# A gated mix of a recurrent attention block and a GEGLU block: one projection group fewer, and all items of a segment in a new order

## The chip, the cores and the metric

The kernel runs on one core of a Trainium2 chip. The time is the device time of one execution in microseconds, as the median of several runs. The profile is one further execution taken with the hardware profiler. PE is TensorE's matmuls and PEld its weight loads, DVE is VectorE, ACT is ScalarE, POOL is GpSimd, and SP only issues DMAs here.

## The reference

`x` has 2048 rows of 640. `g * a + (1 - g) * b` is returned, with `g` a sigmoid gate per row, `b` a GEGLU block (640 to 1536 and back) and `a` an attention that runs over 64 segments of 32 rows. Each segment has 8 memory rows in front, and its new memory comes out of its own attention, so that segment s+1 cannot begin before segment s has ended:

```
for s in range(64):
    h = concat([mem, x[:, 32*s:32*s+32]], axis=1)            # 40 rows
    q, k, v = (einsum('btd,dhe->bhte', h, W) for W in (Wq, Wk, Wv))   # 32 heads of 192
    scores = where(mask, einsum('bhqe,bhke->bhqk', q, k) * 192**-0.5, -1e9)
    o = einsum('bhqk,bhke->bhqe', softmax(scores), v)
    o = einsum('bhte,hed->btd', o, Wo)
    mem = o[:, :8].copy()
    outs.append(o[:, 8:])
```

## The kernel before

A first part (to about 178 us of the span) computes the GEGLU block for all rows, stores `b` in DRAM, loads the attention's weights into SBUF and prepares gates and the first inputs. After it comes `segment(s)` (line 1314) for the 64 segments, all instructions written out.

**Inside a segment.** The 32 heads are taken in four head groups 0 to 3, of eight heads each. The weights of one head group and one matrix are five pieces of 128x1536 (k = 0 to 4). A list `PROG` (line 518) gives the order of the segment's items, and `segment` emits them one by one; each engine runs what it gets in just this order. There is no scheduler: `_Sched` (line 50) only works out which semaphore each instruction must wait for. The items are:

- `("g", n, k)`: row k of projection group n (`proj`, line 1039). `GROUPS` (line 517) says which projections share a group, as pairs of matrix (0 Q, 1 K, 2 V) and head group. For each member there are four matmuls of 384 columns side by side, one for each 32-column strip of the array. All members multiply the same 128x32 input, so only the first member loads weights into the array (line 1061); the others go through `_matmul_kept` (line 226) and keep them. One PSUM bank is taken for each member at k = 0 (`misc_bank`, line 1012, the one longest unused). At k = 4 ScalarE evacuates each member (Q and K at line 1081, V at line 1084), in the group's order. In kind-0 segments (s mod 4 = 0) V is also computed for the rows left over from four segments ("Vl", line 1074).
- `("tq", i)` and `("tk", i)`: VectorE transposes Q or K of head group i (line 1095); for Q, GpSimd makes a copy, Qz (line 1098). There is one buffer for all Q and one for all K.
- `("sc", i)`: mask and scores on TensorE (lines 1106 to 1121), then maximum and subtraction on VectorE (1133, 1135). GpSimd fills in the memory columns of the next head group.
- `("ex", i)`: exponential on ScalarE (1145), sum, reciprocal and products on VectorE (1147 to 1152).
- `("pt", i)`: the probabilities are transposed on TensorE ("pT", lines 1168 and 1173) and evacuated by ScalarE (1186; for the last head group 1180, with VectorE's 1182 beside it).
- `("pv", i)`: the value product on TensorE (1201, 1203), evacuated by ScalarE (1212; the last head group's third part by VectorE, 1217).
- `("wo", i, h)`: half of the output projection of head group i (1230; 1253 for the last group).
- `("lf", q, u, k)` and `("le", q, u, m)`: in segments with s mod 4 = q, Q and K of rows that a later four segments need ("left" rows, line 899), and their evacuation and store (lines 904, 906, 1300, 910). `("vb", k)`: a V row of the same sort, in kind 3 (line 1034).

At the end of a segment VectorE adds up the result and transposes the new memory into the next segment's input (lines 1395, 1399); the next segment's first row waits for that.

**Weights.** Not all weights fit in SBUF. Thirteen pieces of Q, K and V and three of Wo share their places with those of the opposite head group. The head groups are taken forwards in even segments and backwards in odd ones, and as soon as a shared piece has been used for head group 0 (in the order of the segment), SP issues the load of the piece for head group 3 into the same place (`swap_loads`, line 624; 384 KB each, 480 KB for Wo). All DMAs of the segments stand on SP's queue.

The places in the text: "sc2" is the scores of head group 2, "pT2" the first transposing matmul of its probabilities, "K2" its K projection, "the last Wo pairs" line 1253. Head groups are numbered in the segment's own order.

```
    GROUPS = [[(0, 0), (1, 0)], [(2, 0), (0, 1), (1, 1)], [(2, 1), (0, 2)], [(1, 2)], [(2, 2), (0, 3)], [(1, 3)], [(2, 3)]]
    for n, (m, i) in enumerate(ms):                     # in proj: the members of a group
        S_.add("pe", mms(m, bk, htile(k), k, g_, n > 0), ...)   # n > 0: the array's weights are kept
```

Of the kernel before, what the change touches and what calls it, by code (L numbers as in the profile page):

```python
# [238 lines left out]
def _build(nc, A_x, A_mem0, A_Wq, A_Wk, A_Wv, A_Wo, seg_len, w_gate, w_up, w_down,  # L239
# [272 lines left out]
    def piece_view(key, o):  # L512
        if key[0] == 3:
            return bview(o, GO).rearrange("p (c n) -> p c n", n=Dm)
        return bview(o, GQ)

    GROUPS = [[(0, 0), (1, 0)], [(2, 0), (0, 1), (1, 1)], [(2, 1), (0, 2)], [(1, 2)], [(2, 2), (0, 3)], [(1, 3)], [(2, 3)]]
    PROG = [("g", 0, 0), ("g", 0, 1), ("g", 0, 2), ("g", 0, 3), ("g", 0, 4), ("tq", 0), ("g", 1, 0), ("tk", 0),
# [13 lines left out]
    assert NOCT == 4  # L532
    WOP = 4
    NWP = NT
# [4 lines left out]
    def octet(s, i):  # L539
        return i if s % 2 == 0 else NOCT - 1 - i  # L540
# [5 lines left out]
    def seg_order(s):  # L546
        keys = []
        for item in PROG:
            if item[0] == "g":
                keys += [(m, octet(s, i), item[2]) for m, i in GROUPS[item[1]]]  # L550
            elif item[0] == "wo":
# [487 lines left out]
    def proj(s, item):  # L1039
        ms = GROUPS[item[1]]  # L1040
        k = item[2]
# [233 lines left out]

    assert PROG.index(("g", [n for n, ms in enumerate(GROUPS) if (2, 1) in ms][0], KT - 1)) < PROG.index(("wo", 0, 0))
    late_at = ("g", 1, KT - 1)
# [7 lines left out]
    at = PROG.index  # L1285
    k_end, v_end = [max(at(("g", n, KT - 1)) for n, ms in enumerate(GROUPS) if mi in ms) for mi in ((1, NOCT - 1), (2, NOCT - 1))]
    for x, u in mids:
# [26 lines left out]
    def segment(s):  # L1314
# [3 lines left out]
        for n, item in enumerate(PROG):  # L1318
            kind, i = item[0], item[1]
            if kind == "g":  # L1320
# [5 lines left out]
                proj(s, item)  # L1326
                ki = [j for m, j in GROUPS[i] if m == 1 and item[2] == KT - 1]
                kind, i = ("k", ki[0]) if ki else ("", 0)
# [116 lines left out]
def bass_gated_mix__memory_aug_recurrent_mem_tr__glu_gated_geglu__prompt_kernel(  # L1445
    nc,
    A_x,
    A_mem0,
    A_Wq,
    A_Wk,  # L1450
    A_Wv,
    A_Wo,
    A_seg_len,
    B_x,
    B_w_gate,
    B_w_up,
    B_w_down,
    gate_w,
    out,
):  # L1460
    _build(nc, A_x, A_mem0, A_Wq, A_Wk, A_Wv, A_Wo, A_seg_len, B_w_gate, B_w_up, B_w_down, gate_w, out)
# [33 lines left out]
```

## Time and profile before

| | us |
|---|---|
| median of 3 runs (1767.09 to 1770.34) | 1770.06 |
| profiled execution | 1771.21 |
| its span | 1769.4 |
| busy: PE, PEld | 1606.2, 798.4 |
| busy: DVE, ACT, POOL | 959.9, 803.3, 400.6 |
| read from HBM, written | 473.22 MB, 21.11 MB |
| mean busy share of the DMA engines, 130 to 1769 us | 0.80 |
| granted TensorE clock | 0.997 |

A busy PE is not PE at its peak: the ends of matmuls are modelled and overlap. A wait row reads "engine line waited for: us in total, times, longest us". A group row reads "line engine op out<-in xcount | busy us, mean ns of one | idle us before, and what ended it". A timeline row gives start, length, engine, line and operation, and in brackets the idle time ahead of it and what ended that; "issue" means that nothing which the profile shows ended it.

Positions inside a segment are counted from the first matmul of its first projection row. "Kind" is s mod 4; the kinds differ in their left rows and in kind 3's second use of Wo. Instructions of TensorE are counted as matmuls plus weight loads.

### The profile page before, as it was taken

Reading aid. Unit: us, or ns where it says so; the run is one execution under the profiler, and the core shown is the slowest. Engines: PE = TensorE matmul, PEld = TensorE weight load, DVE = VectorE, ACT = ScalarE, POOL = GpSimd, SP = SyncE. Lnnn points to the kernel's source line nnn. Section 1 sums busy time; section 2 is a strip of 40 time slices with the busy share of each in tenths; the row PEclk is TensorE's granted clock in tenths of the full one; section 3 lists DMA queues with packets and bytes.
Section 4 is the critical chain, followed back from the end, with each engine's and each line's share of the span. In section 5 each row is a group of like instructions: output and inputs, shape, how many; then the busy total and the mean of one; then the engine's idle time right before and its main releaser. Section 6 shows DMA issues by size and latency. Waiting matters only on the chain.

```text
span 1769.4 us, 80660 instructions
## 1 busy us (share of the span) xinstructions
PE 1606.2 (91%) x39162; PEld 798.4 (45%) x31501; DVE 959.9 (54%) x2934; ACT 803.3 (45%) x1835; POOL 400.6 (23%) x1358
## 2 busy tenths in 40 slices
PE   9999899989998999889999998988998899989987
PEld 4554444444444444444444444444444444444443
DVE  2222655556565655556555555555565655655554
ACT  3222544545444544445444544444444454444443
POOL 1100222222222222222222222222222222222222
PEclk9999999999999999999999999999999999999999
DMA  9914987888778887878778886878787887879776
GB/s 319 310 45 153 328 314 258 318 306 292 275 271 310 298 312 254 308 289 313 279 273 293 306 314 226 318 283 300 275 284 288 296 315 259 312 276 326 283 277 236
DMA packets 271313, 499.58 MB, mean 282 GB/s; under 512 B 105304, under 2 KB 132208, under 8 KB 270960
## 3 DMA queue, kind: packets, MB, share of 16 engines
q1 hardware_dynamic: 267832, 491.34, 78.2%
q8 instruction: 276, 4.52, 1.0%
q10 hardware_dynamic: 3128, 3.09, 0.5%
q14 instruction: 77, 0.63, 0.1%
HBM read 473.22 MB, written 21.11 MB: 279 GB/s over the span
## 4 chain that ended last, share of the span: by engine, by line
PE 66%; DVE 17%; issue 6%; DMA 5%; ACT 4%; POOL 1%; DVEq 0%; SPq 0%; ACTq 0%; POOLq 0%
PE ps L1061 18%; PE ps L226 14%; PE ps L1230 8%; DMA arena<-in_A_Wo_dram 4%; PE ps L818 3%; PE ps L1201 3%; PE ps L815 3%; PE ps L899 3%; DVE ps L1135 2%; PE ps L1106 2%; DVE arena L1133 2%; PE ps L833 2%; DVE arena L1147 2%; PE ps L1253 2%; DVE arena L1095 2%
## 5 line engine op out<-in xcount | busy, mean ns | idle before, releaser
L1061 PE MATMUL ps<-arena 128*32 128x384 bf16 x9940 | 727.7, 328 | 52.2 <-DVE arena L1399 33.6
L226 PE MATMUL ps<-arena 128*32 128x384 bf16 x7680 | 595.3, 327 | 7.8 <-DVE arena L1239 3.5
L1061 PEld LDWEIGHTS ps<-arena 128*32 128x32 bf16 x9940 | 259.5, 97 | 377.0 <-issue 238.3
L1095 DVE STREAM_TRANSPOSE arena<-arena 128x384 bf16<-128x384 bf16 x512 | 270.6, 557 | 151.3 <-ACT arena L1081 150.3
L1081 ACT ACTIVATE arena<-ps 128x384 bf16<-128x384 f32 x512 | 236.2, 489 | 213.6 <-PE ps L1061 193.2
L1230 PE MATMUL ps<-arena 128*32 128x320 bf16 x6144 | 294.7, 300 | 15.1 <-issue 12.4
L1145 ACT ACTIVATE ps<-ps 104x160 f32<-104x160 f32 x256 | 71.9, 281 | 285.3 <-DVE ps L1135 285.3
L1230 PEld LDWEIGHTS ps<-arena 128*32 128x32 bf16 x6144 | 163.3, 96 | 76.8 <-issue 19.2
L1133 DVE TENSOR_REDUCE arena<-ps 104x4 f32<-104x160 f32 x256 | 82.9, 324 | 163.0 <-PE ps L1121 163.0
L1212 ACT ACTIVATE arena<-ps 128x480 bf16<-128x480 f32 (+1 forms) x256 | 137.0, 535 | 42.5 <-PE ps L1203 37.8
L1098 POOL COPY arena<-arena 64x160 bf16<-64x160 bf16 x256 | 81.3, 318 | 325.3 <-DVE arena L1095 314.2
L1186 ACT ACTIVATE arena<-ps 128x448 bf16<-128x448 f32 x192 | 104.2, 543 | 99.7 <-PE ps L1173 99.1
L1220 POOL COPY arena<-arena 128x96 bf16<-128x96 bf16 x256 | 68.2, 266 | 356.8 <-ACT arena L1212 267.6
L1084 ACT ACTIVATE arena<-ps 128x384 bf16<-128x384 f32 x256 | 125.1, 489 | 26.4 <-PE ps L1061 21.1
L1147 DVE TENSOR_REDUCE arena<-ps 104x4 f32<-104x160 f32 x256 | 83.0, 324 | 93.4 <-ACT ps L1145 93.4
L1201 PE MATMUL ps<-arena 128*64 128x160 bf16 x1536 | 122.1, 242 | 12.1 <-ACT arena L1186 5.8
L1201 PEld LDWEIGHTS ps<-arena 128*64 128x64 bf16 x1536 | 80.8, 109 | 89.1 <-issue 31.6
L899 PE MATMUL ps<-arena 128*32 128x384 bf16 x1280 | 112.7, 332 | 2.4 <-issue 2.4
L956 POOL COPY arena<-arena 128x96 bf16<-128x96 bf16 x256 | 70.3, 275 | 194.1 <-PE ps L1121 130.2
L1203 PE MATMUL ps<-arena 128*64 128x64 bf16 x1536 | 104.8, 194 | 3.9 <-issue 3.9
L1239 DVE TENSOR_TENSOR arena<-ps,arena 64x160 f32<-64x160 f32 x160 | 50.8, 317 | 75.2 <-ACT arena L1236 60.9
L906 DVE STREAM_TRANSPOSE arena<-arena 128x384 bf16<-128x384 bf16 x128 | 73.7, 576 | 31.7 <-ACT arena L904 27.5
(88 smaller groups left out, 2040.7 us busy)
## 6 DMA issues: line engine op xcount, KB each, us to landing
arena<-in_A_Wk_dram SPq DMA_DIRECT2D x335, 384.0 KB, 7.3
arena<-in_A_Wv_dram SPq DMA_DIRECT2D x335, 384.0 KB, 9.1
arena<-in_A_Wo_dram SPq DMA_DIRECT2D x205, 480.0 KB, 6.4
arena<-in_A_Wq_dram SPq DMA_DIRECT2D x209, 384.0 KB, 5.1
arena<-left_qk_scratch SPq DMA_DIRECT2D x126, 96.0 KB, 3.0
left_qk_scratch<-arena SPq DMA_DIRECT2D x49, 192.0 KB, 2.4
left_qk_scratch<-arena SPq DMA_DIRECT2D x30, 96.0 KB, 5.9
ffn_b_scratch<-arena ACTq DMA_DIRECT2D x16, 160.0 KB, 3.8
```

The source lines that it names most:

```text
L226: return e.add_instruction(mybir.InstMatmult(name=nm, start_tensor_calc=like["start"], stop_tensor_calc=stop, tile_size=(128, 32), tile_po ...
L899: fns.append(lambda e, outp=outp, rhs=rhs, j=j: e.matmul(outp, lhs, rhs, start=(k == 0), stop=(k == KT - 1), tile_position=(0, 32 * j)))
L1061: fns.append(lambda e, outp=outp, rhs=rhs, j=j: e.matmul(outp, lhs, rhs, start=(k == 0), stop=(k == KT - 1), tile_position=(0, 32 * j)))
L1081: S_.add("act", lambda e, m=m, bk=bk: e.activation(out=rows_sb[m], in_=ps[:, bk, 0:384], func=ACTF.Copy), reads=[r_ps[bk]], writes=[r_rows ...
L1084: S_.add("act", lambda e, i=i, bk=bk: e.activation(out=v_sb[i % NVB].rearrange("p (c n) -> p c n", c=3), in_=ps[:, bk, 0:384].rearrange("p ...
L1095: S_.add("dve", lambda e: e.transpose(out=dst[:, :, 0:L], in_=rows_sb[m].rearrange("p (c r) -> p c r", r=L)), reads=[r_rows[m]], writes=[r ...
L1133: S_.add("dve", lambda e: e.tensor_reduce(out=mxs, in_=S3, axis=AX.X, op=ALU.max), reads=[rb], writes=[rst], name="smax max")
L1147: S_.add("dve", lambda e: e.tensor_reduce(out=sms, in_=S3, axis=AX.X, op=ALU.add), reads=[rb], writes=[rst], name="smax sum")
L1201: return [lambda e: e.matmul(full, v[:, e0:e0 + 64], PTm[:, i], start=True, stop=False, tile_position=(0, 64 * i), skip_group_check=True), ...
L1203: lambda e: e.matmul(part, vl[:, e0:e0 + 64], PTl[:, i], start=False, stop=True, tile_position=(0, 64 * i), skip_group_check=True)]
L1212: S_.add("act", lambda e: e.activation(out=apx(u[:, 0, 0, :], [[R, na], [3 * R, 4], [1, R]]), in_=ps[:, A, 0:na * W].rearrange("p (c t r) ...
L1230: fns.append(lambda e, i=i, t=t, j=j, gv=gv: e.matmul(ps[32 * j:32 * j + 32, bank, 0:2 * DJ].rearrange("p (h n) -> p h n", h=2), lhs2[i], ...
```

## The change

Two tables change and nothing else. K of head group 2 is no longer a group of its own but the third member of the group with V of head group 1 and Q of head group 2, so that there are six groups instead of seven; it takes a bank at the same time as the other two, and its twenty matmuls run with kept weights. And `PROG` lists all items in a new order. In it "sc" of head group 1 is followed directly by "pv" of head group 0, and "sc" of head group 3 by "pv" of head group 2 (before, "sc" of 2 was followed by "pv" of 1, in kind 1 with a left row between). The rows of V of head group 3 stand nearer to each other, most left rows come earlier, and the last "wo" half is now the last item, so that all "le" items are emitted ahead of the segment's end.

```
-    GROUPS = [[(0, 0), (1, 0)], [(2, 0), (0, 1), (1, 1)], [(2, 1), (0, 2)], [(1, 2)], [(2, 2), (0, 3)], [(1, 3)], [(2, 3)]]
+    GROUPS = [[(0, 0), (1, 0)], [(2, 0), (0, 1), (1, 1)], [(2, 1), (0, 2), (1, 2)], [(2, 2), (0, 3)], [(1, 3)], [(2, 3)]]
     PROG = [("g", 0, 0), ("g", 0, 1), ("g", 0, 2), ("g", 0, 3), ("g", 0, 4), ("tq", 0), ("g", 1, 0), ("tk", 0),
             ("g", 1, 1), ("g", 1, 2), ("sc", 0), ("g", 1, 3), ("ex", 0), ("g", 1, 4), ("tq", 1), ("g", 2, 0),
-            ("g", 2, 1), ("g", 2, 2), ("lf", 1, 0, 0), ("pt", 0), ("g", 2, 3), ("tk", 1), ("g", 2, 4), ("g", 3, 0),
-            ("sc", 1), ("g", 3, 1), ("lf", 1, 0, 1), ("g", 3, 2), ("ex", 1), ("g", 3, 3), ("g", 3, 4), ("g", 4, 0),
-            ("lf", 1, 0, 2), ("pv", 0), ("lf", 1, 0, 3), ("g", 4, 1), ("tk", 2), ("g", 4, 2), ("pt", 1), ("g", 4, 3),
-            ("tq", 2), ("g", 4, 4), ("sc", 2), ("ex", 2), ("lf", 1, 0, 4), ("pv", 1), ("g", 5, 0), ("le", 1, 0, 0),
-            ("g", 5, 1), ("lf", 0, 1, 0), ("g", 5, 2), ("wo", 0, 0), ("le", 1, 0, 1), ("tq", 3), ("pt", 2), ("g", 5, 3),
-            ("wo", 0, 1), ("g", 5, 4), ("pv", 2), ("tk", 3), ("lf", 0, 1, 1), ("lf", 1, 1, 0), ("wo", 1, 0), ("sc", 3),
-            ("lf", 2, 1, 0), ("wo", 1, 1), ("g", 6, 0), ("lf", 2, 1, 1), ("lf", 1, 1, 1), ("g", 6, 1), ("ex", 3),
-            ("g", 6, 2), ("wo", 2, 0), ("lf", 1, 1, 2), ("pt", 3), ("g", 6, 3), ("lf", 2, 1, 2), ("g", 6, 4),
-            ("wo", 2, 1), ("lf", 2, 1, 3), ("lf", 1, 1, 3), ("pv", 3), ("lf", 0, 1, 2), ("lf", 2, 1, 4), ("lf", 1, 1, 4),
-            ("vb", 0), ("le", 1, 1, 0), ("vb", 1), ("vb", 2), ("vb", 3), ("le", 1, 1, 1), ("le", 2, 1, 0),
-            ("lf", 0, 1, 3), ("lf", 0, 1, 4), ("wo", 3, 0), ("le", 2, 1, 1), ("le", 0, 1, 0), ("wo", 3, 1), ("le", 0, 1, 1),
-            ("vb", 4)]
+            ("tk", 1), ("g", 2, 1), ("pt", 0), ("g", 2, 2), ("g", 2, 3), ("g", 2, 4), ("sc", 1), ("pv", 0),
+            ("g", 3, 0), ("tq", 2), ("g", 3, 1), ("g", 3, 2), ("g", 3, 3), ("ex", 1), ("lf", 1, 0, 0), ("tk", 2),
+            ("g", 3, 4), ("lf", 1, 0, 1), ("pt", 1), ("g", 4, 0), ("sc", 2), ("lf", 2, 1, 0), ("ex", 2), ("g", 4, 1),
+            ("lf", 1, 0, 2), ("pv", 1), ("lf", 1, 0, 3), ("lf", 2, 1, 1), ("lf", 1, 0, 4), ("lf", 2, 1, 2),
+            ("g", 4, 2), ("le", 1, 0, 0), ("g", 4, 3), ("tq", 3), ("le", 1, 0, 1), ("lf", 2, 1, 3), ("g", 4, 4),
+            ("tk", 3), ("lf", 0, 1, 0), ("wo", 0, 0), ("wo", 0, 1), ("pt", 2), ("g", 5, 0), ("g", 5, 1),
+            ("lf", 1, 1, 0), ("wo", 1, 0), ("sc", 3), ("pv", 2), ("lf", 1, 1, 1), ("lf", 0, 1, 1), ("g", 5, 2),
+            ("wo", 1, 1), ("ex", 3), ("g", 5, 3), ("lf", 2, 1, 4), ("wo", 2, 0), ("g", 5, 4), ("vb", 0), ("pt", 3),
+            ("lf", 1, 1, 2), ("lf", 0, 1, 2), ("wo", 2, 1), ("pv", 3), ("lf", 1, 1, 3), ("lf", 1, 1, 4),
+            ("lf", 0, 1, 3), ("lf", 0, 1, 4), ("le", 2, 1, 0), ("vb", 1), ("vb", 2), ("vb", 3), ("le", 0, 1, 0),
+            ("vb", 4), ("wo", 3, 0), ("le", 1, 1, 0), ("le", 0, 1, 1), ("le", 1, 1, 1), ("le", 2, 1, 1), ("wo", 3, 1)]
```

All line numbers behind these tables are one smaller in the changed kernel.

## The prediction

> **What bounds the kernel now.** I read the page from the top, then the waits, the groups, the timeline segment by segment, and the order of the instructions in the two programs. On the page:
>
> ```profile
> span 1769.4 us, 80660 instructions
> ...
> PE 1606.2 (91%) x39162; PEld 798.4 (45%) x31501; DVE 959.9 (54%) x2934; ACT 803.3 (45%) x1835; POOL 400.6 (23%) x1358
> ...
> q8 instruction: 276, 4.52, 1.0%
> ...
> PE 66%; DVE 17%; issue 6%; DMA 5%; ACT 4%; POOL 1%; DVEq 0%; SPq 0%; ACTq 0%; POOLq 0%
> ```
>
> TensorE is on two thirds of the chain, VectorE's answers on 17%, and 6% is "issue", where TensorE waits for nothing that the profile shows. From the start of the first segment to that of the last, 63 segments take 1560 us, 24.8 each. I call them kind 0 to 3 by s mod 4; their means are 25.05, 24.88, 23.47 and 25.64 us. Each span starts with Q0's first row. Adding, for each pair of neighbouring items, the shortest spacing of that pair anywhere in the timeline gives TensorE's own work: 21.16, 20.27, 18.55 and 21.11. So some 4.5 us a segment are waits; the order of the items can only move those.
>
> ```profile
> ACT ps L1145 <- DVE ps L1135: 285.3, 256, 3.4
> PEld ps L1061 <- issue: 238.3, 819, 2.6
> PEld ps L1168 <- DVE arena L1152: 82.1, 148, 1.0
> ```
>
> The third row is TensorE's wait for a finished softmax (pT after the last "smax p"). By place, as the mean idle time ahead of an item beyond that shortest spacing, the waits that the new order touches are (kinds 0/1/2/3, us): pT2 .66/.42/.92/.54; sc2 0/.07/.29/.31; sc3 of kind 2 .24; pT0 of kinds 2 and 3 .25; the value product of group 2 in kind 1 .46; the last Wo pairs .06/.53/.54/.17.
>
> The second wait is instruction supply. The 276 packets of queue 8 carry 16 KB each, and 39162+31501 TensorE instructions over 276 are 256: one packet per 256 instructions. Between the first and last segment 75 gaps over 350 ns between matmuls have no semaphore behind them; every one lies at the same place of the 256. One:
>
> ```profile
> 1008.96 0.27 PEld L1061 LDWEIGHTS ps<-arena 128*32 128x32 bf16 x9 [1.29 <-issue]
> ```
>
> No border is passed sooner than 2.18 us after the packet that holds what follows it began. From 3.5 to 18 us of a segment, while 13 weight pieces queue on the DMA rings, that packet begins 3.66 us (median) after a late passing of the border before; after 19 us only 1.2. So in the middle a block costs up to 3.66+2.3=5.96 us: 43 instructions/us. It binds there: 59% of the middle borders are passed within 0.25 us of that limit. From 3.5 us to pT3 all four kinds run at 44 to 46.5 instructions/us, whatever their items.
>
> **The change part by part.** *One group fewer.* Five rows of four weight loads go per segment, 1280 in all.
>
> ```profile
> L1061 PE MATMUL ps<-arena 128*32 128x384 bf16 x9940 | 727.7, 328 | 52.2 <-DVE arena L1399 33.6
> L226 PE MATMUL ps<-arena 128*32 128x384 bf16 x7680 | 595.3, 327 | 7.8 <-DVE arena L1239 3.5
> ```
>
> Rows with a load and rows without follow each other at 0.162 us alike, so time on the array is unchanged; it saves 20 of 1104 instructions, counted below. [...]
>
> *Scores beside a value product.* Projection to scores takes 0.265 us, scores to projection 0.30, projection to value product 0.265, but scores straight to value product 0.203. Each such place saves 0.2. The new order has two per segment (1|0, 3|2), the old one (2|1) in three kinds of four. Item by item TensorE's own work becomes 21.07, 19.98, 18.46 and 20.92: 10.5 us less over all segments. It is contained in the sums below.
>
> *Waits that go.* The shortest scores-to-pT chain is 2.4 us (sc2 at 10.94, pT2 at 13.47). Between sc2 and pT2 stood 1.82/1.94/1.42/1.83 us of work, now 2.58/3.15/3.48/2.99: pT2's wait goes. So do the listed sc2, sc3 and kind-1 waits: about 62 us.
>
> *Waits that come.* ScalarE takes its work in order:
>
> ```profile
> L1081 ACT ACTIVATE arena<-ps 128x384 bf16<-128x384 f32 x512 | 236.2, 489 | 213.6 <-PE ps L1061 193.2
> L1212 ACT ACTIVATE arena<-ps 128x480 bf16<-128x480 f32 (+1 forms) x256 | 137.0, 535 | 42.5 <-PE ps L1203 37.8
> L1145 ACT ACTIVATE ps<-ps 104x160 f32<-104x160 f32 x256 | 71.9, 281 | 285.3 <-DVE ps L1135 285.3
> L1084 ACT ACTIVATE arena<-ps 128x384 bf16<-128x384 f32 x256 | 125.1, 489 | 26.4 <-PE ps L1061 21.1
> ```
>
> Before, two evacuations (V1, Q2) stood ahead of group 1's exponential; now V1, Q2, K2 and the value product's (0.57). From V1's last row: 0.39 to the evacuation, 3x0.52, 0.60, exp 0.31, sum 0.36, reciprocal 0.21, products 0.42, hand-over 0.06: 3.9 us to pT1. Behind that row lie 3.85/3.46/2.82/2.82 us of work. So pT1 waits 0.05/0.43/1.07/1.07, and everything behind it on TensorE with it. K2 needs a bank when V0 is barely out of its own: V0's evacuation ends 1.07 us after V0's last row starts, K2's first row comes at 0.81, a wait of 0.26 in kinds 1 to 3 (in 2 and 3 it replaces pT0's). Group 2's K transpose now stands behind softmax 1 on VectorE: sc2 may wait .14.
>
> *DMAs.* SP issues the 13 pieces and 3 Wo pieces in the old order (kind 1: a left store ahead of the Wo pieces, kind 0: one ahead of a staging load). V3's rows 0 and 1 now stand together and earlier. In kind 1 row 1 lands 15.9 us into the segment and would be wanted at 15.1; but kind 1 is pinned at its end: the last Wo piece lands at 23.5 and 1.1 us follow, so it stays within -0.15 to +0.6. I take 0, for the scores behind V3 wait for their transposes anyway. POOL's copies shift with their producers; none ends a wait named here.
>
> **The sum.** It runs by pT3, the last softmax's first use, behind which a fixed chain follows. Before, pT1 and pT3 stood at 10.95 and 19.84 (kind 0), 9.68 and 18.46 (2), 9.57 and 19.92 (3). Now pT1 comes at its own work plus the waits ahead (sc0 .16, banks .26, in kind 0 .41 for the left bank): 11.7, 10.9, 10.9. From there to pT3 stand 416, 412 and 480 instructions. With no wait for a block they take their work (7.05, 7.08, 7.65) and .3, .3, .24 of small waits: pT3 at 19.05, 18.3, 18.8. With every block at the limit of 43/us they take 9.65, 9.6 and 11.15: 21.35, 20.5, 22.05. In the old order the same two ends can be made: kind 2 had 6.53 of work and 1.58 of waits (17.8), or 384 instructions at the limit (18.6), and stood at 18.46, a share f=.82 of the way; kind 0 at .37, kind 3 at .64, mean .61. For the new order I take half, since during pT1's wait the fetch gets ahead: 20.2, 19.4, 20.4, later than before by .36, .91, .50.
>
> Behind pT3 the tail shrinks: work ahead of the last value product falls from 1.36/1.61/1.37 to 1.13/.74/1.15, but its probabilities need 0.9 (pT and pTl 0.33, evacuation 0.44, two hand-overs); the last Wo pairs come 1.18 behind that product whatever stands between (kind 1: 0.65 of work, 0.53 of wait). By bounds from nothing to these differences I give the tail -.3, -.5, -.22; kind 0 loses .15 again, since a left transpose now precedes the segment's last evacuation on VectorE. Net +.21, +.41, +.28, kind 1 zero: 16x0.90 = +14 us. The profiled execution took 1771.2, so 1785; it lies 1.2 over the median, so 1784.
>
> Every 0.01 of f moves the sum by 1.25 us (16 x .01 x the three distances 2.3, 2.2, 3.25); zero is at f=.385.
>
> **The rivals.** *Faster: the fetch gets ahead.* Should the quiet microsecond at pT1 put the fetch a whole block ahead, f falls to .3 and the removed waits win: -11, 1759. For it: early in a segment packets begin soon after the border. Against: at 10.9 us the rings are full, and the old order had its own waits there. It decides below f=.385. Chance .17. [...] As a mechanism of this kernel it would be f=0: 125x.385=48 us less, 1722, chance .03.
>
> *Heavier: f as before.* The blocks pace the middle as they did, f=.61: +28, 1798. Chance .23.
>
> *V3's second row* in kind 1 is not absorbed: 16x.6 more, 1794. Chance .05.
>
> *Nothing:* f near .385, 1770. Chance .07. That the merge doesn't happen is excluded: the program has 1280 fewer loads.
>
> **How the numbers follow.** My forecast, f from .42 to .57 (+4 to +23), has .45. Slower .45+.23+.05=.73; faster .17+.03=.20; same .07, with 0.2% (3.5 us) what a measurement here can tell. The range goes from f=.35 (-5, 1765) to f=.63 (+31, 1801).
>
> **What would show it.** Right: pT1's idle time near 1 us in kinds 2 and 3 with exp directly behind the value product's evacuation; pT2's and sc2's waits gone; K2's first row waiting for V0's evacuation; 5 packets fewer on queue 8 with "issue" waits as large as before; pT3 later than 19 us in kind 2. Wrong: pT3 earlier than before in kinds 0 and 3, or "issue" halved.

## The result and the profile after

The changed kernel takes 1785.97 us (median of 7 runs, 1776.88 to 1798.51), against 1770.55 for the kernel before in the same comparison: a ratio of 1.0101, 95% interval [1.0065, 1.0138]. It is 1% slower, within 2 us of the forecast of 1784. The profiled execution took 1798.51, so what its segments say adds up to more than the median.

From the page of the changed kernel: the span, the engines' busy time, the packets of instructions, and the chain that ended last.

```profile
span 1796.7 us, 79433 instructions
...
PE 1596.5 (89%) x39181; PEld 776.8 (43%) x30221; DVE 957.2 (53%) x2934; ACT 781.6 (44%) x1835; POOL 400.1 (22%) x1358
...
q8 instruction: 271, 4.44, 1.0%
...
PE 68%; DMA 14%; DVE 7%; ACT 6%; issue 5%; POOL 0%; DVEq 0%; ACTq 0%; SPq 0%; POOLq 0%
```

1280 weight loads and 5 packets are gone, and TensorE is busy 10 us less (1596.5 after 1606.2). VectorE's answers fell from 17% of the chain to 7%, the waits that the new order was to remove. DMA rose from 5% to 14%. So TensorE does less, waits less for the softmax, and still ends later.

The waits of TensorE's weight loads in the changed kernel, with total us, times and longest:

```profile
PEld ps L1060 <- issue: 305.5, 933, 1.5
...
PEld ps L1167 <- DVE arena L1151: 61.2, 112, 0.9
PEld ps L1229 <- issue: 41.0, 60, 3.0
...
PEld ps L1252 <- DMA arena<-in_A_Wo_dram: 18.6, 22, 2.7
```

The first row (projection rows, no semaphore) was 238.3 before and the second (pT for a softmax) 82.1. The third (the output projection of head groups 0 to 2, no semaphore) and the last (the last Wo pairs, whose weights have not landed) were, before:

```profile
PEld ps L1230 <- issue: 19.2, 15, 1.9
...
PEld ps L1253 <- DMA arena<-in_A_Wo_dram: 7.6, 14, 1.0
```

The waits for the softmax fell by 21 us; the other three rows rose together by 100. They are no sum of lost time, as weight loads stand idle while matmuls run (of the 1796.7 us PE is busy 1596.5 and PEld 776.8), but the last two name places: output projections whose instructions or weights come late. What the first row's rise means is told by the runs without transfers.

By kinds of segment, worked out from the timeline as in the prediction (means over the segments from the fifth on, us; "behind" is from pT3 to the next segment's start):

| kind | length before, after | pT3 before, after | behind before, after |
|---|---|---|---|
| 0 | 25.05, 25.87 | 19.84, 20.38 | 5.21, 5.49 |
| 1 | 24.87, 25.22 | 19.76, 19.68 | 5.11, 5.54 |
| 2 | 23.47, 23.76 | 18.46, 18.99 | 5.01, 4.77 |
| 3 | 25.64, 25.71 | 19.92, 20.54 | 5.72, 5.17 |

And one thing that the prediction does not have. The view by stretches of the changed kernel: the stretch; its length; busy time (and instructions) of PE, PEld, DVE, ACT, POOL; the granted clock; the DMA share and GB/s. The second stretch ends a segment of kind 2, the third begins the next one.

```profile
954.17:957.59 3.42, 3.20 (x80) 1.66 (x74) 1.84 (x7) 1.58 (x4) 0.55 (x2) 1.00 0.96 366
957.59:961.00 3.41, 1.58 (x64) 1.18 (x64) 2.63 (x9) 1.64 (x4) 1.14 (x3) 1.00 0.38 130
961.00:964.41 3.41, 3.41 (x48) 0.84 (x20) 0.50 (x2) 0.54 (x2) 0.66 (x3) 0.50 0.86 242
964.41:967.83 3.42, 3.33 (x90) 0.97 (x42) 2.22 (x7) 1.24 (x4) 0.84 (x3) 1.00 0.90 280
```

From 961.00 to 964.41 TensorE was granted half its clock: 48 matmuls in place of about 80 in such a stretch. The two waits that made the stretch ahead thin, in the timeline of PE:

```profile
959.18 1.01 PE L1252 MATMUL ps<-arena 128*32 128x160 bf16 x48 [1.20 <-DVE arena L1216]
960.83 0.38 PE L1060 MATMUL ps<-arena 128*32 128x384 bf16 x4 [0.64 <-DVE arena L1398]
961.00 0.53 PE L226 MATMUL ps<-arena 128*32 128x384 bf16 x4
961.30 0.55 PE L1060 MATMUL ps<-arena 128*32 128x384 bf16 x4
961.62 0.55 PE L226 MATMUL ps<-arena 128*32 128x384 bf16 x4
```

TensorE waits 1.20 us for the last value product's evacuation ahead of the last Wo pairs and 0.64 for the next segment's memory rows; the projection rows that follow stand 0.32 us apart instead of 0.162. Between the first and the last segment start, 12 such stretches lie in this profile and 3 in that of the kernel before. In each profile all begin on one grid of 3.413 us, and in the changed kernel TensorE was busy for 0.09 to 0.48 of the stretch ahead of each.

### The profile page after: what moved, and what is told of

Read it like the earlier page. It is cut to its first block, busy times and chain, and to the rows that moved or that the text cites. A ratio compares the mean times of both kernels' runs of the same rounds, so it can differ in the third digit from the quotient of the medians.

```text
span 1796.7 us, 79433 instructions
## 1 busy us (share of the span) xinstructions
PE 1596.5 (89%) x39181; PEld 776.8 (43%) x30221; DVE 957.2 (53%) x2934; ACT 781.6 (44%) x1835; POOL 400.1 (22%) x1358
## 4 chain that ended last, share of the span: by engine, by line
PE 68%; DMA 14%; DVE 7%; ACT 6%; issue 5%; POOL 0%; DVEq 0%; ACTq 0%; SPq 0%; POOLq 0%
PE ps L1060 17%; PE ps L226 16%; PE ps L1229 10%; DMA arena<-in_A_Wo_dram 6%; DMA arena<-in_A_Wk_dram 4%; DMA arena<-in_A_Wv_dram 4%; PE ps L814 3%; PE ps L817 3%; PE ps L1200 3%; PE ps L898 3%; PE ps L832 2%; PE ps L1252 2%; PE ps L1105 2%; ACT arena L1083 2%; ACT arena L1080 2%
## 5 line engine op out<-in xcount | busy, mean ns | idle before, releaser
L1060 PEld LDWEIGHTS ps<-arena 128*32 128x32 bf16 x8660 | 233.4, 97 | 440.7 <-issue 305.5
L1080 ACT ACTIVATE arena<-ps 128x384 bf16<-128x384 f32 x512 | 229.7, 491 | 278.5 <-PE ps L1060 261.3
L1094 DVE STREAM_TRANSPOSE arena<-arena 128x384 bf16<-128x384 bf16 x512 | 274.4, 559 | 135.5 <-ACT arena L1080 135.5
L1229 PEld LDWEIGHTS ps<-arena 128*32 128x32 bf16 x6144 | 172.6, 97 | 109.0 <-issue 41.0
L1083 ACT ACTIVATE arena<-ps 128x384 bf16<-128x384 f32 x256 | 125.1, 489 | 198.1 <-PE ps L1060 186.0
L1200 PE MATMUL ps<-arena 128*64 128x160 bf16 x1536 | 118.0, 240 | 7.8 <-issue 5.7
L1252 PE MATMUL ps<-arena 128*32 128x160 bf16 x3072 | 76.9, 237 | 47.4 <-DVE arena L1216 27.3
L1252 PEld LDWEIGHTS ps<-arena 128*32 128x32 bf16 x3072 | 57.0, 98 | 77.7 <-DVE arena L1216 24.4
```

The lines of the kernel that those rows point to most:

```text
L1060: fns.append(lambda e, outp=outp, rhs=rhs, j=j: e.matmul(outp, lhs, rhs, start=(k == 0), stop=(k == KT - 1), tile_position=(0, 32 * j)))
L1080: S_.add("act", lambda e, m=m, bk=bk: e.activation(out=rows_sb[m], in_=ps[:, bk, 0:384], func=ACTF.Copy), reads=[r_ps[bk]], writes=[r_rows ...
L1083: S_.add("act", lambda e, i=i, bk=bk: e.activation(out=v_sb[i % NVB].rearrange("p (c n) -> p c n", c=3), in_=ps[:, bk, 0:384].rearrange("p ...
L1094: S_.add("dve", lambda e: e.transpose(out=dst[:, :, 0:L], in_=rows_sb[m].rearrange("p (c r) -> p c r", r=L)), reads=[r_rows[m]], writes=[r ...
L1200: return [lambda e: e.matmul(full, v[:, e0:e0 + 64], PTm[:, i], start=True, stop=False, tile_position=(0, 64 * i), skip_group_check=True), ...
L1229: fns.append(lambda e, i=i, t=t, j=j, gv=gv: e.matmul(ps[32 * j:32 * j + 32, bank, 0:2 * DJ].rearrange("p (h n) -> p h n", h=2), lhs2[i], ...
```

## The experiments

Each ratio is to the kernel before, run on the same chip in the same comparison. The idle time "at borders" is the sum, over all borders between packets of 256 TensorE instructions (69402 over 271 packets in the changed kernel's profile) from the first to the last segment start, of the gap to the next instruction, less a fixed 62 ns for each. The kernel before has 62.4 us of it with 79 gaps over 350 ns, the changed one 81.1 with 78.

### Without the weights' transfers

```
 def swap_loads(seg, item):      # in both kernels
 ...
-            load_piece(other, "swap s%d" % seg)
+            loaded[slot_id[other]] = other
```

The old order:

> The kernel before, with the 16 weight transfers of each segment that exchange one head group's pieces for the next one's left out (each segment multiplies by the pieces that already lie in the memory, so the numbers that come out are of other weights; every instruction of the engines stays). Theory A (the weights queued on the DMA rings delay the packets that bring TensorE's instructions, and so pace the middle of a segment): the packets after 3.5 us of a segment begin about 1.2 us after a late border, as they do behind 19 us, instead of 3.66; the 75 gaps over 350 ns without a semaphore fall below 30, the page's 'issue' wait ahead of the projections from 238 us to below 190, and the time from 1770 to 1700-1735. Theory B (the supply of instructions has nothing to do with the weights, or does not set the end): 1760-1772, with the gaps where they were.

The new order:

> The changed kernel with the same 16 weight transfers of each segment left out (again the numbers that come out are of other weights; every instruction of the engines stays). Theory A (the new order loses because its middle runs at the pace of the instruction packets, while its own work is 10.5 us less and its waits for operands fewer): without the weight queue the new order is no longer slower; against the old order without the transfers it comes out between 15 us faster and 2 us slower. Theory B (it loses by its own waits: pT1 behind the value product's evacuation, K2's bank, the last Wo pairs, none of which the transfers touch): it stays 10 to 20 us slower than the old order without the transfers. Theory C (it loses by the windows of half clock that follow a thin end of a segment): it stays slower by about 1.4 us for each such window that it has more (9 more in the two profiles, 12 us), and the count of windows says so.

Measured: 1695.0 us for the old order, ratio 0.9581 [0.955, 0.9612], and 1676.2 for the new one, 0.9468 [0.9428, 0.9509]. The chains of the old and of the new order:

```profile
PE 69%; DVE 22%; ACT 5%; issue 3%; POOL 1%; DMA 0%; DVEq 0%; POOLq 0%; ACTq 0%
```

```profile
PE 78%; DVE 10%; ACT 9%; issue 2%; DMA 0%; ACTq 0%; POOL 0%; DVEq 0%; POOLq 0%
```

Without the transfers the sign turns: the new order is 19 us (1.1%) faster, a little beyond what theory A gave. At the borders none (old order) and 2 (new order) of the gaps over 350 ns are left. From 3.5 to 18 us of a segment the next packet begins 0.2 us (old) and 0.3 us (new) after a border is passed, as the median; with the transfers it is 3.3 us in both orders. In the segments' means the old order has 24.14, 23.63, 22.84 and 23.42, the new one 23.75, 23.57, 22.42 and 23.39. So theory B (the new order loses by its own waits) is out, and so is theory C as the whole of it: the new order still has 6 stretches at half clock here, the old one 2, and is faster all the same. Two expectations missed: the old order's time lies 5 us below theory A's range, and the "issue" wait ahead of the projections fell only from 238 to 214 us. That row, in the old and in the new order without the transfers:

```profile
PEld ps L1061 <- issue: 214.3, 797, 0.8
```

```profile
PEld ps L1060 <- issue: 291.2, 930, 0.8
```

So most of it is no late packet, and its rise from 238.3 to 305.5 in the changed kernel is none either: it is as large, 77 us, where the packets are not late.

The transfers cost the old order 72 us and the new one 110. This pair does not say by which of their effects, for the waits on weights that land late went with them.

### More weight loads

```
-            S_.add("pe", mms(m, bk, htile(k), k, g_, n > 0),
+            S_.add("pe", mms(m, bk, htile(k), k, g_, n > 0 and (m, i) != (1, 2)),   # changed kernel
+            S_.add("pe", mms(m, bk, htile(k), k, g_, False),                        # kernel before
```

> The changed kernel, with K2's five rows loading their weights again in place of keeping those that V1's rows loaded: 20 more instructions per segment for TensorE, 5 more packets on queue 8, nothing else. Theory A (instructions pace the middle): 20 instructions at 43 per us are 0.47 us a segment where the limit binds, half to three fifths of that by my share: +0.25 us x 63 = +16 us, between +10 and +29. Theory B (a load beside a matmul costs nothing and the supply of instructions does not bind): within 4 us of the changed kernel.

> The kernel before, with every projection row loading its weights, also where it follows a row with the same ones: 25 rows of 4 loads more per segment, 100 instructions, 25 packets more over the run, no other work. Theory A: some 100 instructions at 43 per us, 2.3 us a segment at the limit and 1.4 at a share of .61: +90 to +145 us. Theory B (loads are hidden beside the matmuls, which follow each other at 0.162 us with a load and without): within 10 us of before.

Measured: 20 loads more per segment in the new order 1780.33 us, 1.0068 [1.0043, 1.0093], no more than the changed kernel's 1.0101; 100 more in the old order 1802.91, 1.0193 [1.016, 1.0226], 34 us more. The first puts theory A's rise of 10 us and more out. The second is neither theory: it is a quarter to two fifths of what theory A said, and it sits where that theory puts it (borders' idle time 62 to 105 us, for 25 packets more). A limit of 43 instructions per us that holds for every instruction in the middle of a segment is too strict; in these runs 25 packets cost 1.4 us each.

### One part of the change at a time

The new order with K2 as a group of its own, and the old order with K2 merged:

```
-    GROUPS = [..., [(2, 1), (0, 2), (1, 2)], ...]
+    GROUPS = [..., [(2, 1), (0, 2)], [(1, 2)], ...]      # five rows behind ("g", 2, 4)
...
-    GROUPS = [..., [(2, 1), (0, 2)], [(1, 2)], ...]
+    GROUPS = [..., [(2, 1), (0, 2), (1, 2)], ...]        # old PROG without its ("g", 3, k)
```

> The new order without the merge: K2 is a group of its own again, its five rows right behind those of V1 and Q2, its evacuation behind its own rows, all other items as in the changed kernel (20 weight loads per segment more). Theory A (the merge brings two waits: K2's first row on V0's bank, 0.26 us in three kinds, and pT1 behind one more evacuation, 0.47 us in kinds 2 and 3, some 27 us in all, of which about half reaches the end since the instruction packets pace the middle anyway): both waits are gone from the trace and the time falls by 8 to 18 us, to 1768-1778, although five more packets are fetched. Theory B (the order alone costs, the merge nothing): 1782-1790.

> The merge without the new order: K2's rows stand beside those of V1 and Q2 and keep their weights, the other items stay in the old order. Theory A: K2 takes a bank that V0 has barely left (0.26 us in kinds 1 to 3) and group 1's exponential comes behind one more evacuation; five packets fewer save about one us: +2 to +12 us on before, 1770-1780. Theory B (the merge is free and its 1280 loads were a cost): 1755-1766.

Measured: the order alone 1781.41 us, 1.0097 [1.0069, 1.0124], the merge alone 1766.28, 1.0013 [0.9988, 1.0037]. The whole loss is the order's. The merge is not free of waits, it is paid back. In its trace:

```profile
PEld ps L1058 <- issue: 259.1, 781, 1.2
...
PEld ps L1165 <- DVE arena L1149: 110.3, 161, 1.1
...
PEld ps L1250 <- DMA arena<-in_A_Wo_dram: 12.2, 13, 2.4
```

pT now waits 110 us for softmaxes (82.1 before), 0.32, 0, 0.69 and 0.68 us a segment ahead of pT1, and K2's first row waits 0.26 in three kinds: some 40 us of new waits. The borders' idle time went from 62.4 to 15.2. So some 40 us of waits came, 47 at borders went, and the two nearly cancel. I read it so that packets catch up during a wait ahead of the middle, and operands during a packet's lateness; the trace shows the sums, not this. In the order alone the same is seen from the other side: K2's wait is gone, pT1's fell to 0.3, and pT0 waits 0.5 in all kinds instead.

### The exponential ahead of the value product

```
-    ("sc", 1), ("pv", 0), ..., ("g", 3, 3), ("ex", 1),
+    ("sc", 1), ("ex", 1), ("pv", 0), ..., ("g", 3, 3),
```

> The changed kernel with group 1's softmax issued directly behind its scores, ahead of the value product of group 0, so that on ScalarE the exponential no longer stands behind that product's evacuation (0.57 us). Theory A: pT1's wait (0.47 us in kinds 2 and 3) goes from the trace; between a half and all of 32x0.47 = 15 us reaches the end: 1771-1780. Theory B (the packets of instructions take the gain back, as pT1's wait is time in which the fetch gets ahead): 1782-1788 with the wait gone and the border gaps larger.

Measured: 1782.86 us, 1.0113 [1.0074, 1.0152]. pT1's wait fell only from 0.47 to 0.26 us in kinds 2 and 3: the exponential starts 0.17 us earlier, right behind the subtraction on VectorE, so the value product's evacuation had held it no longer than that. And sc2 waits 0.49 there, for GpSimd's copy of group 2's transposed Q, since VectorE now does that transpose behind softmax 1. The time is theory B's, but not for its reason: the wait moved on by one item.

### The thin end of a segment

The view by stretches again, now the last 3.41 us of segment 30 (kind 2) and the first of the next. Before:

```profile
941.28:944.69 3.41, 2.26 (x64) 1.02 (x56) 2.57 (x8) 1.35 (x4) 1.14 (x3) 1.00 0.26 80
944.69:948.10 3.41, 3.41 (x77) 0.94 (x33) 1.68 (x5) 0.87 (x2) 0.97 (x4) 1.00 0.82 205
```

After:

```profile
957.42:960.83 3.41, 1.58 (x62) 1.18 (x62) 2.49 (x8) 1.64 (x4) 1.14 (x3) 1.00 0.43 148
960.83:964.24 3.41, 3.41 (x48) 0.94 (x24) 0.64 (x3) 0.37 (x1) 0.66 (x3) 0.53 0.79 223
```

TensorE is busy for 2.26 of those 3.41 us in the old order and for 1.58 in the new one. Over all positions 0.4% of the old order's stretches of 3.41 us are busy for less than half, and 2.8% of the new one's; with some 457 stretches in the segments that makes 2 and 13, where 3 and 12 at half clock are seen. First, two rows of the left projection moved to the end:

```
-    ..., ("lf", 2, 1, 4), ("wo", 2, 0), ..., ("lf", 0, 1, 2), ("wo", 2, 1), ("pv", 3),
+    ..., ("wo", 2, 0), ..., ("wo", 2, 1), ("pv", 3), ("lf", 0, 1, 2), ("lf", 2, 1, 4),
```

> The changed kernel with two of the left projection's rows moved from ahead of the last value product to behind it (the last of kind 2 and the third of kind 0), where they cover the wait of the last Wo pairs for that product's evacuation (1.17 us in kind 2, 0.4 in kind 0, against 0.54 and 0.06 in the old order). Theory A (this wait is lost time, and the thin stretch brings the windows of half clock at the start of the next segment): the wait falls below 0.7 and to 0.1, the windows inside segments from 12 to at most 6, the time by 10 to 20 us, to 1766-1776. Theory B (what ends a segment is the landing of the last Wo piece or the next segment's first operands): the wait goes and the idle time turns up ahead of the next wait; within 5 us of the changed kernel.

Measured: 1778.94 us, 1.0078 [1.0049, 1.0107]. The wait ahead of the last Wo pairs fell from 1.17 to 0.76 us in kind 2 and from 0.38 to 0.14 in kind 0; in kind 0 the two waits beside it (PV3, the next segment's first row) took it over. The gain on the changed kernel, 4 us, is smaller than the intervals. The profiled execution has 4 stretches at half clock, but it is the fastest of the seven (1765.63 us, clock 0.995); the mean clock over the seven is 0.991, so theory A is not borne out and the time is within theory B's 5 us.

Then the stretch was filled without moving any work:

```
+        if q < 3 and s + 1 < NSEG:
+            fb = max((b for b in (0, 1, 2, 3) if b not in lb.values()), key=lambda b: misc[b])
+            S_.add("pe", [... identity x identity, 128x512, into bank fb ...] * 3, name="filler s%d" % s)
         mix(s)
```

> The changed kernel with three idle matmuls (identity by identity, 128x512, into a bank that is free) behind the last Wo pair of each segment of kinds 0, 1 and 2, where TensorE otherwise waits 0.8 to 1.0 us for the next segment's first operand; 6 instructions more per such segment. In the trace of the changed kernel the clock goes by stretches of 3.41 us on a fixed grid, and a stretch in which TensorE was busy for less than about half is followed by one at half clock; the last 3.41 us of its segments of kind 2 are busy for 0.47 to 0.49 (0.74 in the old order), those of kind 1 for 0.51 (0.60). Theory A (these stretches cost some 1.5 us each and are most of the loss): the busy share there rises by 0.64/3.41 = 0.19, the windows at half clock fall from 12 to 4 or fewer, the mean clock from 0.989 to 0.996 or more, and the time by 9 to 17 us, to 1768-1777. Theory B (the windows fall into time in which TensorE waits anyway, or the clock follows something else): the clock or the time stays, within 4 us.

> The kernel before with the same three idle matmuls per segment. Theory A: the old order has few thin stretches (0.4% of all 3.41 us stretches under one half, against 2.8% in the new order; mean clock 0.997), so there is little to win: between 4 us faster and 2 us slower than before. Theory B (idle matmuls help whatever the windows do, or hurt by their instructions): 5 us or more away from before on either side.

Measured: the new order with idle matmuls 1774.11 us, 1.0024 [0.9999, 1.0049], 14 us better than the changed kernel's 1.0101; the old order with them 1769.27, 1.0003 [0.9978, 1.0028], nothing. The time is as theory A said. The clock is not: its mean over the runs rose from 0.989 to 0.992, not to 0.996, and the profiled execution (1784.65 us) still had 10 stretches at half clock, though most of them now lie in kind 3, where no idle matmuls stand. A stretch lowers the mean by 0.5x3.41/1780 = 0.00096; so 11 became 8, and at about 1.4 us each (32 matmuls of 80 missing) that is 4 to 5 us of the 14. Where the other 9 come from these runs do not settle.

### Fewer weights in flight

```
+        if name.startswith("swap"):
+            inflight[0] += 1
+            turn = [Rg("turn", inflight[0] % 3, inflight[0] % 3 + 1)]
-        S_.add("sp", ..., writes=[r_res[key]],
+        S_.add("sp", ..., writes=[r_res[key]] + turn,
```

> The changed kernel with at most three of the exchange transfers of weights in flight: each waits on its queue until the third before it has landed. Instructions and bytes are the same. Theory A (TensorE's instruction packets begin late because of the depth of the weight queue: 3.3 us after a late border in mid-segment, 1.1 us behind 19 us): packets in mid-segment begin within 2.5 us, the idle time at block borders falls from 81 us to below 45, and the time by 5 to 20 us unless the later weights make waits of their own, which the trace then names. Theory B (it is that transfers run at all, not how many are queued): the delay stays at 3 us or more, and the time is that of the changed kernel or, with weights that land later, 5 to 30 us longer.

Measured: 1965.86 us, 1.1091 [1.1057, 1.1125]. Its chain:

```profile
DMA 51%; PE 41%; DVE 4%; ACT 3%; issue 1%; SPq 1%; POOLq 0%; ACTq 0%; DVEq 0%; POOL 0%
```

Half of the chain now runs through weight transfers. TensorE's own waits for them:

```profile
PE ps L1066 <- DMA arena<-in_A_Wv_dram: 110.9, 128, 3.0
PE ps L1258 <- DMA arena<-in_A_Wo_dram: 73.1, 79, 2.6
```

The idle time at borders is gone (gaps over 350 ns there: 1 in place of 78), and in mid-segment the next packet begins 1.2 us after a border in place of 3.3, as theory A said. But three transfers in flight move the weights too slowly, and the waits for V's and Wo's pieces, 184 us, are about as large as the loss. TensorE also takes 1966 us for the instructions that it ran in 1786, and so passes its borders more slowly; the depth of the queue is not shown clean of that. The loss, some 180 us, is far beyond what either theory gave.

### Real work at the end

```
     kind 2: ("lf", 2, 1, 2) in the place of ("lf", 2, 1, 4); ("lf", 2, 1, 3), ("lf", 2, 1, 4) behind ("pv", 3)
     kind 0: ("lf", 0, 1, 1) in the place of ("lf", 0, 1, 2); ("lf", 0, 1, 2) behind ("pv", 3)
+    the three idle matmuls of the run above
```

> The changed kernel with the three idle matmuls behind the last Wo pair (kinds 0 to 2) and, beside them, real work moved to the thin end: in kind 2 two rows of the left projection, in kind 0 one, go from the middle of the segment to behind the last value product, where they stand in the wait for its evacuation (1.17 us in kind 2, 0.4 to 0.5 in kind 0). Theory A (idle time at the end is lost, and the middle, which gives the rows up, keeps its pace): the wait ahead of the last Wo pairs falls below 0.4 us in kind 2 and to 0.15 in kind 0, 16x(0.8+0.3) = 18 us, of which a half to all reaches the end, and the windows at half clock become fewer: 1756-1767 on a chip where before takes 1768, as fast as the old order or up to 12 us faster. Theory B (the middle's rows were no cost either, since TensorE waits there for something else, and the last weights or the next segment's operands end the segment): the wait goes and turns up at the last Wo piece or the next segment's first row; within 4 us of the run with idle matmuls alone (1774).

Measured: 1756.42 us against 1761.92 on its chip, ratio 0.9981 [0.9957, 1.0005], 1.2% under the changed kernel's ratio and level with the old order. The same two stretches, the end of segment 30 and the start of the next:

```profile
935.20:938.61 3.41, 2.91 (x75) 1.22 (x59) 2.61 (x8) 1.51 (x4) 0.83 (x3) 1.00 0.30 94
938.61:942.02 3.41, 3.41 (x80) 0.98 (x37) 1.74 (x5) 0.87 (x2) 1.38 (x5) 1.00 0.59 127
```

2.91 us busy in place of 1.58, and 80 matmuls at full clock in place of 48. The wait ahead of the last Wo pairs is 0.46 us in kind 2 (1.17; below 0.4 was expected) and 0.16 in kind 0 (0.38). 4 stretches at half clock are left in its profile, and the mean clock over its runs is 0.996 (0.997 in the old order). Its middle gave up a row in kind 0 and two in kind 2: pT3 comes at 19.78 and 18.44 instead of 20.38 and 18.99. The time lies where theory A put it, no longer than the old order's; theory B would have kept it some 5 us above that. The moved rows were not run without the idle matmuls, nor in the old order.

## Why the prediction was right, and where it was not

**The direction.** The forecast was that waits worth some 62 us go, that others come, and that packets of instructions held up by the weights keep the middle from getting faster. The runs without transfers show the first half: the new order is 1.1% faster when nothing delays packets and weights. That the new order loses in the presence of the weights is shown too. That late packets alone do it is not: the borders' idle time is 19 us larger in the changed kernel's profile, but 54 to 71 us, near the old order's 62, in four kernels with almost the same middle (idle matmuls 71, exponential earlier 64, the two tail variants 58 and 54), and in mid-segment the next packet begins 3.3 us after a border in the old order as in the new one.

**Where the time stands in a segment.** I had 16 x (0.36+0+0.91+0.50) = +28 us ahead of pT3 and 16 x (0.15+0.5+0.22) = -14 behind it. By the table it is +26 ahead and -1 behind, in a profiled execution that is 27 us longer than that of the kernel before, and not 15. So the later middle came, the shorter end did not, and the half-clock stretches, most of which begin with a segment and so lie ahead of pT3, were not in the sum at all. That the median comes within 2 us of the forecast is in part luck.

**The two ends of pT3.** With no wait for a block I had pT3 at 19.05, 18.3 and 18.8 (kinds 0, 2, 3); without transfers it came at 19.21, 18.01 and 18.92. That bound holds within 0.3 (those runs also have no waits for weights). The other end, 43 instructions per us for every block, fell with the extra loads, which should have cost 90 us or more by it and cost 34. The share of one half between the two came out right: 20.38, 18.99 and 20.54 are 0.58, 0.31 and 0.54 of the way, mean 0.48. A step that interpolates between a sound end and a bad one was right as a number, not as a law: the reading that fits is that packets' lateness and waits for operands take each other's place in the middle, as in the merge alone (some 40 us more of waits, 47 less at borders, a ratio of 1.0013).

**The waits.** K2's bank wait is 0.26 in kinds 1 to 3, as worked out. pT2's and sc2's waits went. pT1's is 0.47 in kinds 2 and 3 and nothing in kinds 0 and 1, where I had 1.07, 1.07, 0.05 and 0.43. The step that failed is the addition of whole durations on ScalarE. The timeline of ACT in the changed kernel, a segment of kind 2:

```profile
1045.04 0.49 ACT L1083 ACTIVATE arena<-ps 128x384 bf16<-128x384 f32 x1 [0.60 <-PE ps L1060]
1045.43 0.87 ACT L1080 ACTIVATE arena<-ps 128x384 bf16<-128x384 f32 x2
1046.17 0.59 ACT L1211 ACTIVATE arena<-ps 128x480 bf16<-128x480 f32 x1
1046.62 0.33 ACT L1144 ACTIVATE ps<-ps 104x160 f32<-104x160 f32 x1
```

V1's evacuation starts at 1045.04, the two row evacuations end 0.87 us after the first of them starts, the value product's starts at 1046.17 and the exponential at 1046.62. Evacuations of 0.49 us start some 0.38 apart: each begins before the one ahead has ended. The chain is 3.4 us, not 3.9.

**Behind pT3.** I gave the end -0.15, 0, -0.5 and -0.22 us by kind; it measured +0.28, +0.43, -0.24 and -0.55. In kind 2 I had named the cover (0.74 us of work where 0.9 is needed) and its minimum of 1.18 behind the product, but not its price: the last Wo pairs wait 1.17 there (0.54 before), 0.38 in kind 0 (0.06). In kind 1 the last Wo piece lands too late by 0.99 us (0.43 before): I took that end as pinned and put the risk on V3's second row. Two errors of opposite sign, the too large pT1 wait and this, kept the sum near. The sum also has a slip of its own: for kind 0 it takes 0.3 off the end, where its bounds reach only to 1.36-1.13 = 0.23. And its 1104 instructions a segment count the first part's too; a segment has some 1070.

**The signs.** K2's wait, the 5 packets and "issue" waits no smaller than before came as named, but the last says nothing of the packets, as the runs without transfers show. pT1's wait "near 1 us" is half of that, and pT3 of kind 2, named as later than 19 us, is at 18.99.

**What was not there at all** is the clock. Its mean is 0.997 over the runs of the kernel before and 0.989 over those of the changed one: 7 to 8 stretches more at half clock, about 10 us at 1.4 each. That they cost time is seen in the rows 0.32 us apart (0.162 at full clock); how much of the loss they make is not settled, as the idle matmuls took 14 us away and only 3 stretches. The single executions say that it may be more: by a straight line through the seven of the changed kernel each 0.001 of clock goes with 2.1 us, and in the four sets of 10 to 23 of the kernel before with 1.8 to 2.1. By that the difference in clock would be 13 to 16 us, and the idle matmuls' 0.003 some 6. This is a correlation, and it does not hold everywhere: the new order with K2's loads stands at 0.988 and loses no more than the changed kernel.

**An account, not a proof:** -19 us without transfers, +19 at borders in this profile, +9 for kind 1's last Wo piece (16 x 0.56), +10 for the clock make +19; measured are 18 (1.01% of 1770). Single executions of this kernel differ by 10 us and more, so each term is good to no better than that; the terms overlap as well (the -19 has 4 more half-clock stretches in it already), and the profile that the +19 comes from is 27 us over the one before. So the agreement proves nothing.

**The rivals.** "Faster: the fetch gets ahead" (1759) did not come about with the weights in place. "Heavier" (1798) is excluded for the median by the interval (1782 to 1795), and so is "nothing" (1770). *V3's second row* (1794) lies inside the interval, so the time does not exclude it; in the trace that row waits 0.27 us in kind 1, 4 us in all, where the rival had 0.6. That f can be 0 (1722, chance .03) no run shows: with the weights in place 79 borders of the old order and 78 of the new one have gaps over 350 ns, and without them, where 0 and 2 are left, the new order takes 1676 us.

## What to carry to other kernels

When an order of work is changed, look at the thinnest stretch it leaves on the bounding engine, not only at the waits that it removes: here an order that is faster without the weights in flight left an end of segment in which TensorE was busy for 1.58 of 3.41 us. Idle matmuls and work put into that stretch made up the whole loss (a ratio of 0.9981 in place of 1.0101), though by which of their effects is not shown. The waits here (operands, instruction packets, weights) took turns and did not add up: the merge alone brought some 40 us of them, took 47 away at borders and stands at a ratio of 1.0013. So the price of each is best measured by a run in which its rival is absent. ScalarE's evacuations of 0.49 us, 0.38 us apart, overlap in the profile, so take a chain's steps from start to start.

## What the runs showed of the hardware

- In the profiles of the kernel before and of the changed one the granted clock goes by stretches of 3.413 us on a fixed grid: the 3 and 12 stretches at half clock inside the segments begin on it within 1 ns and are one stretch long each. In the changed kernel TensorE was busy for 0.09 to 0.48 of the stretch ahead of each; the longest idle time in the stretch ahead of 961.00 is 1.2 us. The bound is not sharp: in the same profile stretches busy for 0.46 and 0.48 were not followed by half clock, and in the kernel before stretches busy for 0.46, 0.50 and 0.54 were, and some busy for 0.44 and 0.47 were not.
- In these runs TensorE's instruction packets (queue 8, 16 KB each) came late with the weights' transfers and not without: with them the next packet begins 3.3 us (median, mid-segment) after a border is passed and 79 and 78 borders have gaps over 350 ns; without them it is 0.2 and 0.3 us and 0 and 2 gaps, with the same instructions.
- With at most three of the weights' transfers of 384 or 480 KB in flight the changed kernel takes 1966 us in place of 1786, with 184 us of waits for V's and Wo's pieces.
- Evacuations in a row on ScalarE take 0.49 us each and start 0.386 us apart (median of 369 pairs in the changed kernel, 304 in the kernel before).
